# Weight preparation and temporaries in an adaLN linear-attention and MLP kernel: w2 in turn over eleven products, own value tiles for one block, own tiles for modulated rows, one plain group prepared on GpSimd

## The chip, the cores and the metric

The kernel runs on one core of one Trainium2 chip. The metric is the device time of one execution in microseconds, lower being better. The engines are named as the profile names them: PE (TensorE matmul), PEld (its weight loads), DVE (VectorE), ACT (ScalarE), POOL (GpSimd) and SP (SyncE, which issues the DMAs).

## The reference

One block of a conditioned transformer: a modulation from a vector c, a linear attention and an MLP with SiLU. S is 2048 tokens, D is 576, F is 4608, 32 heads of 18.

```python
mod = (_silu(c) @ w_mod).reshape(c.shape[0], 6, 1, -1)
sa, ca, ga, sb, cb, gb = (mod[:, i] for i in range(6))
h = _layernorm(x) * (1 + ca) + sa
x = x + ga * A(h, A_wqkv, A_wo)
h = _layernorm(x) * (1 + cb) + sb
x = x + gb * (silu(h @ B_w1) @ B_w2)

# A: q, k, v = split(h @ wqkv); phi(t) = where(t > 0, t + 1, exp(t)) + 1e-6
# kv = sum_s phi(k) v; z = sum_s phi(k); o = phi(q) kv / (phi(q) z + 1e-6); return o @ wo
```

## The kernel before, in words

All data are 32-bit. Matmuls keep precision by splitting an operand into a high part of type fp32r (a cast on ACT) and a low part (full minus high, a subtraction, mostly on DVE by the helper `sub_hi` at line 62), and by adding three products: high by high, high by low, low by high.

**First stage (to about 225 us).** Modulation, layer norm and transposition of the first block, then k, v and part of the q projections over 16 token tiles (L154), and the sums kv and z.

**Second stage (the loop over s, lines 751 to 787; about 225 to 460 us).** In round s the denominators of token tile s are made (`prod` on POOL at L760, then `q_norm` on DVE), tile s - 1 is transposed, and tile s - 2 goes through `attn_out`, whose weights M are three tiles of the pool `wp`. Every four tiles a layer norm of one block of 512 tokens is finished, and a generator `turn_all(tb)` is queued. It transposes the block in five chunks and modulates them (`turn_chunk_k`: psum to a temporary by ACT at L127, a cast at L693, a subtraction), makes four sums of quarter blocks per pair of chunks on POOL (L712 to L716), splits these into S, and stores everything to the DRAM tensors `hd`, from where the last stage streams it. After its tail chunk the turn appends "units" of the MLP to a filler list, for two of the 18 groups of 256 hidden units, which are done plainly here: two `mlp_up` (L641, silu at L643 into a temporary, cast into `hs` at L644, subtraction) and four `mlp_down` (L655, added to acc at L657) per group. `new_hs()` has a single buffer, and `temp()` two, named `sl`; the turns, the silu outputs and the late q projections all take `temp()`. The weights of the two plain groups come by `load_mlp` in round 4: for each group a DMA of w1, cast and subtraction, the tail (with a POOL memset of part of `wt`, which lies in unused rows of M[2]), a DMA of w2, a multiplication by gb, cast and subtraction; the raw data go through the one `hs` buffer.

**Last stage (from 459.8 us).** The other 16 groups are taken in 8 pairs d, and each pair of groups is multiplied with each of the four blocks b: 32 units. A unit does a seven-product (Winograd) form of both matmuls: seven products `up` in the order 1, 6, 2, 5, 7, 4, 3 (L911) and seven products `down` in the order 1, 7, 2, 4, 5, 6, 3 (L999); the `down` of a unit runs between the `up` products of the next one. After each `up`, adds on DVE (L929, L936, L950) and a silu on ACT follow; `operands` makes the seven operands of `down`, by DVE and POOL (L957, L958 and the sums L969 to L978, which run on POOL). After each `down`, DVE adds a psum bank to U or acc (L1002). The rows of h are streamed by SP into four `rooms`, one fetch per product (L888).

The class `Weights` prepares a pair's weights, with two raw buffers in the pool `wm`. `load1`, `sums1` and `up` make w1 during the unit b = 3 of the pair before, as the program writes it. `load2` is written at the end of that unit. `sums2(s)`, for each of the two groups s of the pair, multiplies w2 by gb (two DVE instructions at L864) and makes four Winograd sums on POOL (L829 to L832); `split2` then makes the cast (L878) and the subtraction (L62) of one of seven parts. Before the change both `sums2` are written ahead of the first product of unit b = 0, and after product q of that unit `down(n)` splits part n = DOWN[q] of both groups. The parts are first read by the `down` products that run during unit b = 1. `w2p` has eight buffers for these parts.

**What sets the order.** In the last stage the order of PE is the program's own (`manual_schedule` for PE). The order of the other engines, and in the second stage that of PE too, comes from a planner that simulates the program when it is built: among what it believes ready, it takes what was written first, and it moves work forward where the data are there. Each engine then executes its queue strictly in that order.

Of the kernel before, what the change touches and what calls it, by code (L numbers as in the profile page):

```python
# [8 lines left out]
F32 = mybir.dt.float32  # L9
F32R = mybir.dt.float32r  # L10
# [5 lines left out]
P = 128  # L16
# [5 lines left out]
def kernel(ctx: ExitStack, tc, A_x, A_wqkv, A_wo, B_x, B_w1, B_w2, c, w_mod, out):  # L22
# [8 lines left out]
    V, A, G, T = nc.vector, nc.scalar, nc.gpsimd, nc.tensor  # L31
# [3 lines left out]
    S, D = x.shape  # L35
# [4 lines left out]
    NB = S // 512  # L40
    KC = D // P
# [5 lines left out]
    G2 = 2  # L47
    NG = F // (G2 * P)

    def f32(ap):  # L50
        return ap.bitcast(F32)
# [9 lines left out]
    def sub_hi(lo, full, hi):  # L61
        return V.tensor_sub(lo, full, f32(hi))  # L62
# [5 lines left out]
    hTa = tc.alloc_tile_pool(name="hTa", bufs=2)  # L68
    wg = tc.alloc_tile_pool(name="wg", bufs=2)
    wp = tc.alloc_tile_pool(name="w", bufs=3)  # L70
    wqp = tc.alloc_tile_pool(name="wq", bufs=1, side="right")
# [9 lines left out]
    bc = {n: pool.tile([P, D], F32, name=f"bc_{n}") for n, pool in (("ga", pa), ("gb", const))}  # L81
# [333 lines left out]
    for t in range(NT):  # L415
        tb, i = t // 4, t % 4
# [28 lines left out]
        for _ in range((0, 2, 1, 1)[t] if t < 4 else 1):  # L445
            q = next(qs)
# [42 lines left out]
    for j, kv in enumerate(kvp):  # L489
        n = min(2, NHC - 2 * j)  # L490
# [27 lines left out]
    M = [wp.tile([P, 4, D], F32R, name="w") for _ in range(3)]  # L518
# [28 lines left out]
    pc = tc.alloc_tile_pool(name="pc", bufs=1, reuse_waits="tile")  # L547
    wg2 = tc.alloc_tile_pool(name="wg2", bufs=2, reuse_waits="tile")
    px = tc.alloc_tile_pool(name="px", bufs=1, reuse_waits="tile")
# [31 lines left out]
    def new_hs(shape=(P, G2, 2, 512), dtype=F32R):  # L581
        t = pc.tile(list(shape), dtype, name="hs")
        return t

    def load_mlp(g, pool, wt):
        f0 = g * FW
        r1 = new_hs((P, KC + 1, FW), F32)
        nc.sync.dma_start(r1[:, 0:KC, :], B_w1[0 : KC * P, f0 : f0 + FW].rearrange("(k p) f -> p k f", p=P))
        for h in range(2):
            nc.sync.dma_start(r1[h * 64 : h * 64 + 64, KC, :], B_w1[KC * P : D, f0 : f0 + FW])  # L590
        w1 = pool.tile([P, 9, FW], F32R, name="w")
        A.copy(w1[:, 0:KC, :], r1[:, 0:KC, :])
        sub_hi(w1[:, KC : 2 * KC, :], r1[:, 0:KC, :], w1[:, 0:KC, :])
        G.memset(f32(wt[64:128, 1, :]), 0.0)
        tail_w(wt, r1[:, KC, :])
        r2 = new_hs((P, G2, D), F32)
        nc.sync.dma_start(r2, B_w2[f0 : f0 + FW, :].rearrange("(j p) d -> p j d", p=P))
        w2 = pool.tile([P, G2, 2, D], F32R, name="w")
        V.tensor_mul(r2, r2, bc["gb"].unsqueeze(1).to_broadcast([P, G2, D]))
        A.copy(w2[:, :, 0, :], r2)  # L600
        sub_hi(w2[:, :, 1, :], r2, w2[:, :, 0, :])
        return w1, w2, wt


# [21 lines left out]
    def temp():  # L626
        t = pc.tile([P, D], F32, name="sl", bufs=2)
        return t[:, :512]
# [29 lines left out]

    def mlp_units(tb, w):

        hs = new_hs()
        up = [lambda j=j: mlp_up(tb, w[0], w[2], hs, j) for j in range(G2)]
        return up, [lambda i=i: mlp_down(4 * tb + i, hs, w[1]) for i in range(4)]

# [32 lines left out]

    def turn_all(tb):

        nonlocal wqp  # L700
        if tb == 0:
            wqp.release()
            wqp = tc.alloc_tile_pool(name="S", bufs=1, side="right", reuse_waits="tile")
        X = h2[tb] = hTa.tile([P, 2 * KC + 2, 512], F32R, name="hT")

        S = [wqp.tile([P, 4, 2 * HT], F32R, name="S", bufs=2) for _ in range(2)]
        for c in range(2):
            t0, t2 = temp(), temp()
            turn_chunk_k(tb, c, t0)
            turn_chunk_k(tb, 2 + c, t2)  # L710
            (a11, a21), (a12, a22) = ((t[:, :HT], t[:, HT:]) for t in (t0, t2))
            G.tensor_sub(a11, a11, a21)  # L712
            G.tensor_add(a21, a21, a22)
            split_s(S[0], c, t0)
            G.tensor_sub(a22, a22, a11)
            G.tensor_sub(a12, a12, a22)  # L716
            split_s(S[1], c, t2)
            yield
        t = temp()
        turn_chunk_k(tb, KC, t)  # L720
        for w in ws:
            up, down = mlp_units(tb, w)
            filler.extend(up + down)
        G.tensor_sub(t[:, :HT], t[:, :HT], t[:, HT:])
        tail_h(X[:, DIFF, :HT], t[:, :HT])
        yield
        store_h(tb, 1, X[:, 0:4, :HT])
        store_h(tb, 2, X[:, 4:9, :HT])
        store_h(tb, 4, X[:, 4:9, HT:])
        store_h(tb, 5, X[:, 8:9, HT:], 4)  # L730
        store_h(tb, 3, X[:, DIFF : DIFF + 1, :HT], 4)
        for n, at in ((7, 0), (5, HT)):
            store_h(tb, n, S[0][:, :, at : at + HT])
        for n, at in ((3, 0), (6, HT)):
            store_h(tb, n, S[1][:, :, at : at + HT])
        yield

    turns, filler = [], []
    qts, xn2, lns = {}, {}, {}

# [7 lines left out]
            if turns and next(turns[0], StopIteration) is StopIteration:  # L748
                turns.pop(0)

    s = 0
    while s < NT + 5 or filler or turns:
        if s < QB - 2:
            filler.append(late_q)
        if s == 4:
            ws = [load_mlp(g, pool, M[2][:, 1 + g, :512].rearrange("p (a f) -> p a f", a=2))
                  for g, pool in enumerate((wg, wg2))]
        if NP0 <= s < NT:
            prod = pb.tile([P, D], F32, name="prod")
            G.tensor_mul(prod, acc[s], z)  # L760
            pns[s] = q_norm(s, prod, pb.tile([P, DX], F32, name="pn", bufs=2))
        t = s - 2
        if t in (5, 9, 13, 17):
            turns.append(turn_all(t // 4 - 1))
        turn_chunk()
        if 0 <= s - 1 < NT:
            qts[s - 1] = q_transpose(pns.pop(s - 1))
        turn_chunk()
        if 0 <= t < NT:
            attn_out(t, qts.pop(t))  # L770
            tb = t // 4
            if t % 4 == 0:
                lns[tb] = LayerNorm(px)
            lns[tb].stats(t % 4, acc[t])
            if t % 4 == 3:
                lns[tb].finish()
                xn2[tb] = [px.tile([P, DX], F32, name="xn", bufs=4) for _ in range(4)]
                for i in range(4):
                    lns[tb].normalise(i, xn2[tb][i], acc[4 * tb + i], A if tb < 2 or i % 2 else V)
        turn_chunk()  # L780
        unit(1 if s < 8 else 2)
        turn_chunk()
        if s % 4 == 0 and s < NT or s > NT:
            unit()
        s += 1
# [2 lines left out]

    for p in (pb, px, wg2, pc, wp, wg, hTa, wqp):
        p.release()
    psB.release()
    psC = tc.alloc_tile_pool(name="psC", bufs=1, space=PSUM, reuse_waits="tile")
# [16 lines left out]

    class Weights:


        def __init__(self, d):
            self.f0, self.wt, self.w1, self.w2 = 2 * d * FW, wts[d % 2], {}, {}
# [50 lines left out]
                self.split2("B12", s, parts[1])  # L867
            self.b2[s] = self.winograd(*parts, [t[:, i] for i in range(3)])

        def down(self, n):  # L870
            for s in range(2):
                self.split2(n, s, self.b2[s][n])

        def split2(self, n, s, src):
            if n not in self.w2:
# [163 lines left out]
    with tc.manual_schedule(engines={mybir.EngineType.PE}):  # L1039
        w = Weights(1)  # L1040
        for f in (w.load1, w.sums1):
            for s in range(2):
                f(s)
        for n in ORDER:
            w.up(n)
        for s in range(2):
            w.load2(s)
        for i in range(4):
            fetch(i)
        for u in U:  # L1050
            G.memset(u, 0.0)
        ws = {1: w}
        before = None
        for m, (d, b) in enumerate(units):
            unit = Unit(m, ws[d])
            final = m + 1 == len(units)
            if b == NB - 1 and d < ND:
                w = ws[d + 1] = Weights(d + 1)
                for f in (w.load1, w.sums1):
                    for s in range(2):  # L1060
                        f(s)
            if b == 0:
                for s in range(2):
                    ws[d].sums2(s)
            for q, n in enumerate(ORDER):
                unit.up(n)
                if before:
                    before.down(q)
                if final:
                    unit.plain_operands(n)  # L1070
                else:
                    unit.operands(n)
                if b == 0:
                    ws[d].down(Unit.DOWN[q])
                if b == NB - 1 and d < ND:
                    ws[d + 1].up(n)
                if m + 3 == len(units) and q == 3:
                    Unit(len(units) - 1, w).add_u((1, 1), (1, 0), (0, 1))
            if b == NB - 1 and d < ND:
                for s in range(2):  # L1080
                    ws[d + 1].load2(s)
            before = unit
        for t in (2, 3, 0, 1):
            unit.plain_down(t)
# [31 lines left out]
```

## Time and profile before

The three runs took 1252.07, 1256.47 and 1259.71 us; the median is 1256.47.

| what | us |
|---|---|
| median of the runs | 1256.47 |
| the profiled execution | 1249.34 |
| its span, first to last instruction | 1247.6 |
| PE busy | 1176.7 (94%) |
| DVE busy | 841.8 (67%) |
| POOL busy | 551.3 (44%) |
| ACT busy | 490.4 (39%) |
| mean granted clock of PE | 0.985 |

The busy shares are means over three different stages. A line of the windows view gives, for one stretch: its length, then for PE, PEld, DVE, ACT and POOL the busy us and the number of instructions that started in it, the granted clock of PE, the busy share of the DMA engines and what they moved in GB/s. A line of the waits view says which engine waited on which instruction, for how long in total, how often, and the longest. A line of the timeline gives start, duration, engine, line, operation, output and input, and in brackets the idle time before it with what ended it. In the groups, "x66 | 48.9, 771" means 66 instructions, 48.9 us in all, 771 ns each.

### The profile page before, as it was taken

The numbers are of one execution on the slowest core, as the hardware profiler recorded it, in microseconds if no ns is written. First come the engines' busy times: TensorE is split into PE (matmuls) and PEld (weight loads), VectorE is DVE, ScalarE is ACT, GpSimd is POOL, SyncE is SP. The second block draws the span as 40 slices with busy tenths as digits, with TensorE's granted clock in tenths as the row PEclk, the third lists the DMA queues.
The fourth block names the chain that finished last, engine by engine and source line by source line (L and its number), as shares of the span: only waits on it lengthen the run. The fifth ranks groups of instructions, "written<-read, shape, count | busy, mean of one in ns | idle before, by whom it ended". The sixth has DMA issues, their size and how long they took to land.

```text
span 1247.6 us, 21904 instructions
## 1 busy us (share of the span) xinstructions
PE 1176.7 (94%) x8809; PEld 1150.5 (92%) x8809; DVE 841.8 (67%) x1309; ACT 490.4 (39%) x944; POOL 551.3 (44%) x471
## 2 busy tenths in 40 slices
PE   5999999897999969999999998999998999998998
PEld 5999999896999768999999998999998999998998
DVE  6665744995775475577578568569568568667764
ACT  5434342234463333343344244244344334333331
POOL 3200000323231435556457457547637736846560
PEclk9999999998999989999999999999999999999999
DMA  9121300224153626566566566565655755655572
GB/s 297 64 67 58 110 1 1 79 88 154 46 176 119 232 88 236 182 214 198 189 213 203 171 224 191 186 194 196 212 180 196 225 181 190 229 182 191 190 247 99
DMA packets 80452, 202.72 MB, mean 162 GB/s; under 512 B 6682, under 2 KB 37662, under 8 KB 80350
## 3 DMA queue, kind: packets, MB, share of 16 engines
q1 hardware_dynamic: 80350, 201.31, 49.2%
q8 instruction: 70, 1.15, 0.4%
q14 instruction: 32, 0.26, 0.1%
HBM read 179.78 MB, written 21.50 MB: 161 GB/s over the span
## 4 chain that ended last, share of the span: by engine, by line
PE 70%; DVE 15%; DMA 8%; POOL 2%; ACT 2%; issue 2%; SPq 1%; DVEq 0%; ACTq 0%; POOLq 0%
PE up L911 23%; PE down L999 21%; PE psK L154 12%; DMA raw<-in_B_w_dram 6%; PE small L641 4%; DVE w L62 4%; PE big L655 3%; PE big L154 3%; DVE raw L864 3%; PE kvp L389 1%; DVE acc L1002 1%; PE down L1034 1%; DVE h L958 1%; DMA acc<-in_A_wqkv_dram 1%; DVE f L950 1%
## 5 line engine op out<-in xcount | busy, mean ns | idle before, releaser
L999 PE MATMUL down<-w,h 128*128 128x288 f32 x2604 | 384.4, 296 | 17.4 <-DVE U L1002 14.0
L911 PE MATMUL up<-room,w 128*128 128x256 f32 x2688 | 384.9, 286 | 13.8 <-DVE f L929 7.6
L999 PEld LDWEIGHTS down<-w,h 128*128 128x128 f32 x2604 | 357.0, 190 | 20.4 <-DVE U L1002 15.4
L911 PEld LDWEIGHTS up<-room,w 128*128 128x128 f32 x2688 | 353.5, 194 | 16.7 <-DVE f L929 9.4
L969 POOL TENSOR_TENSOR s<-f,f 128x512 f32<-128x512 f32 x31 | 40.1, 1292 | 275.2 <-ACT f L951 275.2
L1002 DVE TENSOR_TENSOR acc<-down,acc 128x576 f32<-128x576 f32 x155 | 116.5, 752 | 59.3 <-PE down L999 58.6
L951 ACT ACTIVATE f<-f 128x512 f32<-128x512 f32 x96 | 60.7, 633 | 197.0 <-DVE f L950 197.0
L154 PE MATMUL psK<-w,hT 128*128 128x288 f32 (+2 forms) x896 | 125.5, 298 | 1.7 <-DVE hT L62 1.1
L154 PEld LDWEIGHTS psK<-w,hT 128*128 128x128 f32 x896 | 121.3, 190 | 2.8 <-DVE hT L62 1.6
L957 ACT CAST h<-f 128x512 fp32r<-128x512 f32 x159 | 95.3, 616 | 52.6 <-POOL f L978 47.7
L911 PE MATMUL up<-room,wt 128*128 128x256 f32 x512 | 104.2, 285 | 0.0
L958 POOL TENSOR_TENSOR h<-f,h 128x512 fp32r<-128x512 f32 x62 | 92.6, 1494 | 12.6 <-ACT h L957 12.6
L958 DVE TENSOR_TENSOR h<-f,h 128x512 fp32r<-128x512 f32 x97 | 80.7, 832 | 16.3 <-ACT h L957 15.1
L62 DVE TENSOR_TENSOR w<-raw,w 128x288 fp32r<-128x288 f32 (+1 forms) x130 | 84.6, 683 | 8.4 <-ACT w L852 8.1
L958 POOL TENSOR_TENSOR h<-s,h 128x512 fp32r<-128x512 f32 x62 | 87.2, 1407 | 0.7 <-ACT h L957 0.7
L911 PEld LDWEIGHTS up<-room,wt 128*128 128x128 f32 x512 | 81.0, 195 | 0.0
L950 DVE TENSOR_TENSOR f<-up,f 128x512 f32<-128x512 f32 x64 | 44.0, 688 | 41.5 <-PE up L911 41.4
L1002 DVE TENSOR_TENSOR U<-down,U 128x576 f32<-128x576 f32 x62 | 46.7, 753 | 31.1 <-PE down L999 31.1
L154 PE MATMUL big<-w,qT 128*128 128x288 f32 x448 | 64.6, 299 | 2.4 <-DVE den L509 1.3
L62 DVE TENSOR_TENSOR w<-t,w 128x256 fp32r<-128x256 f32 (+1 forms) x96 | 64.1, 696 | 2.5 <-ACT w L852 2.1
L655 PE MATMUL big<-w,hs 128*128 128x288 f32 x384 | 58.5, 305 | 6.2 <-ACT hs L644 3.9
L154 PEld LDWEIGHTS big<-w,qT 128*128 128x128 f32 x448 | 60.4, 189 | 3.2 <-DVE qT L62 1.6
(184 smaller groups left out, 1616.0 us busy)
## 6 DMA issues: line engine op xcount, KB each, us to landing
room<-hd SPq DMA_DIRECT2D x128, 640.0 KB, 3.9
room<-hd SPq DMA_DIRECT2D x96, 512.0 KB, 3.7
raw<-in_B_w_dram SPq DMA_DIRECT2D x16, 576.0 KB
hd<-S SPq DMA_DIRECT2D x16, 512.0 KB, 4.5
raw<-in_B_w_dram SPq DMA_DIRECT2D x16, 512.0 KB, 3.7
hd<-hT SPq DMA_DIRECT2D x8, 640.0 KB, 8.0
xt<-in_A_x_dram SPq DMA_DIRECT2D x16, 288.0 KB, 5.6
raw<-in_w_mod_dram SPq DMA_DIRECT2D x8, 576.0 KB, 3.7
```

The costliest lines, as they stand in the source:

```text
L62: return V.tensor_sub(lo, full, f32(hi))
L154: T.matmul(ps, xpart(a), wpart(b), start=n == 0, stop=n == len(XW) - 1)
L641: T.matmul(ps, left, right, start=n == 0, stop=n == len(seq) - 1)
L655: T.matmul(ps[:, h, :HALF], hs[:, j, a, tok], w2[:, j, b, h * HALF : (h + 1) * HALF], start=n == 0, stop=n == len(seq) - 1)
L911: T.matmul(ps[:, s], left, right, start=first and s == 0 and m == 0, stop=m == len(seq) - 1, skip_group_check=True)
L950: V.tensor_add(f, ps, more)
L951: A.activation(f, f, AF.Silu)
L957: A.copy(t[:, 0], src)
L958: eng.tensor_sub(t[:, 1], src, f32(t[:, 0]))
L969: G.tensor_add(s1, f[1, 0], f[1, 1])
L999: T.matmul(ps[:, p, :HALF], self.a[n][:, a, s, tok], self.w.w2[n][:, s, b], start=n in (1, 5, 7, 6) and j == 0, stop=j == 5, skip_group_ch ...
L1002: V.tensor_add(dst, ps[:, :, :HALF], dst)
```

## The change

Four edits.

1. `load_mlp` takes an engine for the two subtractions and the multiplication. Group 0 is prepared in round 4 with DVE as before; group 1 is prepared in round 6 with POOL.
2. In the last block (tb = 3) the two groups' `hs` are two new tiles of the pool `wp`, which take the buffers of M[0] and M[1].
3. A new pool `tp` with two buffers `rows` is opened at the first turn. The temporaries of the first pair of chunks (c = 0) and of the tail chunk come from it; those of the second pair come from `temp()` as before.
4. `Weights.down` becomes `down_step(u)`, with u counting products from the start of unit b = 0 (0 to 13, through unit b = 1). Group s = 0 has its `sums2` at u = 0 and its seven splits at u = 0 to 6; group s = 1 has its `sums2` at u = 4 and its splits at u = 4 to 10.

```diff
-    def load_mlp(g, pool, wt):
+    def load_mlp(g, pool, wt, eng):
...
         A.copy(w1[:, 0:KC, :], r1[:, 0:KC, :])
-        sub_hi(w1[:, KC : 2 * KC, :], r1[:, 0:KC, :], w1[:, 0:KC, :])
+        eng.tensor_sub(w1[:, KC : 2 * KC, :], r1[:, 0:KC, :], f32(w1[:, 0:KC, :]))
...
-        V.tensor_mul(r2, r2, bc["gb"].unsqueeze(1).to_broadcast([P, G2, D]))
+        eng.tensor_mul(r2, r2, bc["gb"].unsqueeze(1).to_broadcast([P, G2, D]))
         A.copy(w2[:, :, 0, :], r2)
-        sub_hi(w2[:, :, 1, :], r2, w2[:, :, 0, :])
+        eng.tensor_sub(w2[:, :, 1, :], r2, f32(w2[:, :, 0, :]))
...
     def mlp_units(tb, w):
 
-        hs = new_hs()
+        hs = new_hs() if tb < NB - 1 else wp.tile([P, 4, D], F32R, name="w").rearrange("p a d -> p (a d)")[
+            :, : 4 * 512].rearrange("p (j h t) -> p j h t", j=G2, h=2)
...
     def turn_all(tb):
 
-        nonlocal wqp
+        nonlocal wqp, tp
         if tb == 0:
             wqp.release()
             wqp = tc.alloc_tile_pool(name="S", bufs=1, side="right", reuse_waits="tile")
+            tp = tc.alloc_tile_pool(name="tp", bufs=1, reuse_waits="tile")
+
+        def rows():
+            t = tp.tile([P, 512], F32, name="rows", bufs=2)
+            return t
...
         for c in range(2):
-            t0, t2 = temp(), temp()
+            t0, t2 = (temp(), temp()) if c else (rows(), rows())
...
-        t = temp()
+        t = rows()
         turn_chunk_k(tb, KC, t)
...
-        if s == 4:
-            ws = [load_mlp(g, pool, M[2][:, 1 + g, :512].rearrange("p (a f) -> p a f", a=2))
-                  for g, pool in enumerate((wg, wg2))]
+        if s in (4, 6):
+            g, pool, eng = ((0, wg, V), (1, wg2, G))[s // 2 - 2]
+            ws.append(load_mlp(g, pool, M[2][:, 1 + g, :512].rearrange("p (a f) -> p a f", a=2), eng))
...
     class Weights:
+        LAG = 4
...
-        def down(self, n):
+        def down_step(self, u):
+
             for s in range(2):
-                self.split2(n, s, self.b2[s][n])
+                v = u - s * self.LAG
+                if v == 0:
+                    self.sums2(s)
+                if 0 <= v < 7:
+                    n = Unit.DOWN[v]
+                    self.split2(n, s, self.b2[s][n])
...
-            if b == 0:
-                for s in range(2):
-                    ws[d].sums2(s)
             for q, n in enumerate(ORDER):
...
-                if b == 0:
-                    ws[d].down(Unit.DOWN[q])
+                if b < 2:
+                    ws[d].down_step(7 * b + q)
```

More of the change, by code (lines that the diff above doesn't have):

```diff
@@ L736, in turn_all @@
         yield
+    tp = None
     turns, filler = [], []
@@ L749, in turn_chunk @@
                 turns.pop(0)
-    s = 0
+    s, ws = 0, []
     while s < NT + 5 or filler or turns:
@@ L785 @@
         s += 1
-    for p in (pb, px, wg2, pc, wp, wg, hTa, wqp):
+    for p in (tp, pb, px, wg2, pc, wp, wg, hTa, wqp):
         p.release()
```

## The prediction

> **What bounds the kernel.** I first cut the span at the places where the program changes stage and asked for each engine's busy time there.
>
> ```profile
> core 0: us, PE busy (x) PEld busy (x) DVE busy (x) ACT busy (x) POOL busy (x), PEclk, DMA share, GB/s
> 225.60:459.80 234.20, 211.09 (x1386) 196.64 (x1384) 168.93 (x303) 99.05 (x175) 73.60 (x74) 0.96 0.38 122
> 459.80:480.00 20.20, 17.52 (x119) 17.32 (x120) 10.74 (x19) 7.00 (x16) 12.18 (x14) 0.83 0.75 256
> 480.00:1231.00 751.00, 725.80 (x5690) 720.32 (x5689) 518.03 (x713) 291.37 (x580) 435.88 (x350) 0.99 0.60 197
> ```
>
> TensorE bounds every stage. The change touches the second stage (attention output, two plain MLP groups; 23.1 us of idle PE) and the streamed stage (25.2 us of idle PE). Nothing can be won outside those idle times and the time lost to a lowered clock. So the next view was what PE waited for, first in 225 to 480 us, then in 480 to 1231 us.
>
> ```profile
> PE small L641 <- ACT sl L127: 5.4, 4, 1.8
> PE small L142 <- ACT sl L127: 4.2, 1, 4.2
> PE big L655 <- ACT hs L644: 3.9, 1, 3.9
> PE up L911 <- DVE acc L657: 3.3, 1, 3.3
> ...
> PE big L655 <- DVE acc L657: 2.3, 1, 2.3
> ```
> ```profile
> PE down L999 <- DVE U L1002: 14.0, 7, 2.1
> PE up L911 <- DVE f L929: 7.6, 7, 1.9
> PE down L999 <- DVE acc L1002: 3.1, 7, 0.4
> ```
>
> Columns: total us, times, longest. The second list is 24.7 us in seven equal portions of 3.5: one for each change from one pair of groups to the next. The timeline of one such place shows the cause.
>
> ```profile
> 647.71 1.97 DVE L864 TENSOR_TENSOR raw<-raw,bc_gb 128x576 f32<-128x576 f32 x2 [2.97 <-DMA raw<-in_B_w_dram]
> ...
> 651.02 3.61 DVE L864 TENSOR_TENSOR raw<-raw,bc_gb 128x576 f32<-128x576 f32 x2
> ...
> 655.52 0.74 DVE L1002 TENSOR_TENSOR U<-down,U 128x576 f32<-128x576 f32 x1
> 656.32 1.62 PEld L999 LDWEIGHTS down<-w,h 128*128 128x128 f32 x12 [2.31 <-DVE U L1002]
> ```
>
> The add of U at L1002 empties a bank that PE had filled by 648.6; it comes at 655.5, because the second group's two multiplications (3.61 us) and other w2 work stand ahead of it in DVE's queue. How much w2 work one unit holds follows from the groups by shape:
>
> ```profile
> L62 DVE TENSOR_TENSOR w<-raw,w 128x288 fp32r<-128x288 f32 x66 | 48.9, 771 | 0.3 <-ACT w L878 0.3
> L864 DVE TENSOR_TENSOR raw<-raw,bc_gb 128x576 f32<-128x576 f32 x32 | 42.4, 1362 | 24.1 <-DMA raw<-in_B_w_dram 24.1
> L62 DVE TENSOR_TENSOR w<-t,w 128x288 fp32r<-128x288 f32 x48 | 33.5, 711 | 0.4 <-ACT w L878 0.4
> ```
>
> A unit with b = 0 gives DVE 4 multiplications x 1.362 + 8 subtractions x 0.771 + 6 x 0.711 = 15.9 us of w2 work, beside 7 adds L1002 x 0.752 + 4 adds into f x 0.687 + 3 splits x 0.832 = 10.5. That is 26.4 us, where an undisturbed unit of PE lasts 23.1 (the same piece of the chain of waits starts at 885.31 and 908.41). The excess, 3.3, is what PE loses, 3.5.
>
> Last, the clock in slices of 5 us:
>
> ```profile
> 290.00:295.00 5.00, 3.64 (x10) 2.13 (x8) 3.20 (x4) 2.73 (x5) 2.63 (x3) 0.50 0.30 105
> 445.00:450.00 5.00, 5.00 (x21) 4.87 (x22) 2.50 (x6) 0.33 (x1) 0.00 (x0) 0.50 0.67 220
> ```
>
> After the waits of 4.2 and 3.9 us the granted clock is one half (the slice 295 to 300 has 0.52), so these waits cost more than themselves.
>
> **Part 1, second plain w on POOL and two rounds later.** DVE loses three operations of 2.27, 1.34 and 1.29 us (at 253.4, 261.2 and 265.5): 4.9 us. POOL gets 1024, 1152 and 1152 elements; its rows at 576 elements take 1.43 us, so 2.54 + 2.86 + 2.86 = 8.3 us. PE was busy all the time from 255 to 280, so DVE's relief is worth nothing directly. The three transfers and the zeroing move with them; group 1's w is first read after group 0's unit, that is behind 300 us, some 30 us after the 267 at which it is ready now. What could queue behind the new POOL work is prod (L760), which is made a round ahead, with DVE's den behind it. Value 0. Upper end 8.3 - 4.9 = +3.4, if all of POOL's time stands in DVE's way; lower end -2, the bit that an earlier layer norm gives the turn.
>
> The Trainium skill, SBUF — State Buffer, section Who interferes with whom, says that a VectorE instruction with two SBUF inputs and a GpSimd one that reads SBUF lock each other out, the later one blocking fully. The trace agrees: the 1024-wide subtraction took 1.21 us alone and 2.27 at 253.4, beside a prod that ran to 254.6. By that rule alone the part would cost the whole 3.4 and the end would be 3.4 us later; I stay at 0 because reductions and PSUM reads, much of DVE's work there, have one SBUF input.
>
> **Part 2, own hs tiles for the last plain block.** Before, all hs are one buffer. At 439.4 the cast L644 has to wait for the products before it, ACT meanwhile takes fourteen casts L852 (439.9 to 444.2), and PE stands 3.90 us, then runs at half clock for 5 us (2.5 lost). With two tiles in M's place (M[0], M[1], last read by attn_out of tile 15, long before) the cast needs only its own silu. -6.4. Ends: 0, if another thing is as late (the casts L852 still have to be made ahead of the first streamed product), and -12, if the two acc L657 waits (3.3 + 2.3) go as well.
>
> **Part 3, rows tiles.** At turn 0, PE waits 4.17 + 1.13 + 1.19 us between 285 and 296, and 290 to 300 runs at half clock (half of 3.64 + 4.04 busy, 3.8 lost). The second c's modulation waited at 288.77 for the first c's tile; it needs only the transposes, done at 285.4. The tail's waited until 295.13; with rows it waits for the first c's split, done at 288.2: up to 6.9 us earlier. POOL's four sums (L712 to L716, 0.73 to 1.18 each) stay in series, so I take 4 of the 6.5 and half of the clock: -6. At turn 3 the same tiles cost PE 1.77 + 1.33; half: -1.5. In turns 1 and 2 PE does not wait. Ends 0 and -13.4.
>
> **Part 4, w2 over eleven products.** Group 1's multiplications, sums and splits are four products later. Of its seven splits the last four (two x 0.771, two x 0.711 = 3.0 us) fall into unit b = 1, where DVE has room (15.1 busy of 25 in 675 to 700). Unit 0 keeps 23.4 against 23.1. The first multiplications still wait for their transfer, so the 0.44 stays; of 3.5 I take 2.4 per change, x 7 = -17. Casts on ACT and sums on POOL move along; raw of group 1 is free four products (13 us) later, so its next load on SP's queue is too, with 30 us to spare before b = 3. Ends: -29 (all 24.7, and 4.75 of clock lost in three slices at 0.93 to 0.95), 0 and worse (rivals).
>
> **Sum.** 0 - 6.4 - 7.5 - 17 = -30.9. The profiled execution took 1249.34 us (span 1247.6), 7.1 below the median of 1256.47. 1249.3 - 30.9 = 1218.4, and 7.1 more: **1225**.
>
> **Rivals**, on the same scale.
> A. The edit doesn't spread anything: DVE's order comes from a planner that moves work forward as soon as its data is there (w1 sums written for b = 3 run at 677, in b = 1). Then unit 0 keeps its 26.4 us, and only parts 2 and 3 count: 1256.5 - 13.9 = 1242.6. Against it: what is written later is ranked behind what is ready too, and the U add would pass.
> B. The second stage keeps its waits: the turn is POOL's chain of sums, and the switch to the streamed stage is held by w1's casts. Only part 4: 1239.5.
> C. The wait moves to POOL. Group 1's four sums (0.89 + 1.07 + 1.03 + 1.02 = 4.0 us) now stand before the operand work of b = 0, whose a[7] is ready at 700.5 in an ordinary unit and read by PE at 701.3: 0.8 of slack. 3.2 us x 8 = 26 back: 1251. Against it: POOL idles 6.8 us ahead of that work (663.0 to 669.9).
> D. Slower: group 1's halves come too late for unit 1. Written at product 4, they take 2 x 1.362 + 0.43 + 0.77 = 3.9 us plus DVE's backlog, and are read at product 7, 9.9 us on; a backlog over 6.0 stalls PE. The f add at L929 was 4.5 behind its releaser in the old order (657.8, 662.3). The part decides against the rest from a backlog of 6.0 + 30.9/8 = 9.9; at 12 it costs 6.0 x 8 = 48 against 30.9: 1274.
>
> **Chances.** Forecast 0.45 (own range 1208 to 1240), A 0.16, B 0.13, C 0.11, D 0.15. What a measurement can tell here is about 0.5%, 6.3 us: faster is below 1250.2, slower above 1262.7. The forecast, A and B are faster, 0.74; C is about no change, 0.11; D is slower, 0.15. The range leaves out D and a little below: 1205 to 1262.
>
> **What would show it.** Part 4: the waits for U L1002 and f L929 under 10 us together, the streamed period (L864 to L864, 97.9 now) near 95; A shows as two pairs of L864 still ahead of the first U add, C as PE waiting for POOL h L958, D as PE waiting for L62 or L878 of w. Part 2: no PE wait on hs L644, clock 1.00 around 440. Part 3: no wait over 2 us on sl L127 or rows. Part 1: PE unbroken from 250 to 285. I am wrong if the streamed stage is not shorter by 10 us, or if a wait of a new name takes more than 10.

## The result, and the profile after

The changed kernel takes 1248.4 us (median of 20 runs) where the kernel before takes 1253.8 (median of 20); the ratio is 0.9955 with a 95% interval of 0.9937 to 0.9972. That is 5.6 us faster, inside what the prediction called no change (its bound was 0.5%), where it had forecast 31 us. (The forecast started from 1256.5, the median of three runs.) The profiled execution took 1246.05 us, its span 1244.2.

The six longest waits of PE from 225 to 480 us, in the changed kernel:

```profile
PE down L1015 <- POOL h L974: 3.8, 1, 3.8
PE small L641 <- DVE hT L62: 3.5, 1, 3.5
PE big L655 <- ACT w L644: 3.4, 1, 3.4
PE up L927 <- ACT p L941: 2.0, 1, 2.0
PE up L927 <- DVE acc L657: 1.6, 1, 1.6
PE up L927 <- DVE f L966: 1.4, 1, 1.4
```

The wait of 4.2 us for the modulation at the first turn (L127) is gone and the acc waits shrank from 5.6 to 1.6. But later in the same turn, at 297.0, PE now waits 3.5 us for a subtraction (hT L62). The cast L644, which part 2 was to free, is still 3.4 us late. And the first streamed unit has two new names, POOL h and ACT p, beside a wait for f that the kernel before had there too:

```profile
PE up L911 <- DVE f L950: 2.7, 1, 2.7
```

The waits from 480 to 1231 us:

```profile
PE down L1015 <- DVE U L1018: 13.9, 7, 2.1
PE up L927 <- DVE f L945: 6.5, 5, 1.9
PE down L1015 <- DVE acc L1018: 3.2, 7, 0.5
```

23.6 us against 24.7: part 4, the largest term of the forecast, did nothing. The timeline of the second change of pairs, in the changed kernel, shows why:

```profile
643.86 1.75 PE L1015 MATMUL down<-w,h 128*128 128x288 f32 x12
...
645.32 1.43 DVE L874 TENSOR_TENSOR raw<-raw,bc_gb 128x576 f32<-128x576 f32 x2 [3.59 <-DMA raw<-in_B_w_dram]
...
648.09 3.61 DVE L874 TENSOR_TENSOR raw<-raw,bc_gb 128x576 f32<-128x576 f32 x2
...
652.59 0.75 DVE L1018 TENSOR_TENSOR U<-down,U 128x576 f32<-128x576 f32 x1
...
653.39 2.82 PE L1015 MATMUL down<-w,h 128*128 128x288 f32 x12 [2.06 <-DVE U L1018]
```

Group 1's two multiplications are written four products later now, yet they stand where they stood: ahead of the first add into U. The product that this add empties ended at 645.6, 2.5 us before they began, so this order was planned and is not one of arrival. DVE's queue there, as the two programs were built (the multiplications of both groups, and what follows):

```
before                              after
raw x gb L864 x2 (group 0)          raw x gb L874 x2 (group 0)
acc L1002                           acc L1018
split h L958                        split h L974
raw x gb L864 x2 (group 1)          raw x gb L874 x2 (group 1)
w minus high L62                    w minus high L62
U L1002                             U L1018
```

### The profile page after: what moved, and what is told of

Same layout as the page of the kernel before. It is cut to its first block, busy times and chain, and to the rows that moved or that the text cites. A ratio compares the mean times of both kernels' runs of the same rounds, so it can differ in the third digit from the quotient of the medians.

```text
span 1244.2 us, 21883 instructions
## 1 busy us (share of the span) xinstructions
PE 1177.2 (95%) x8809; PEld 1151.3 (93%) x8809; DVE 850.5 (68%) x1306; ACT 490.9 (39%) x944; POOL 561.1 (45%) x474
## 4 chain that ended last, share of the span: by engine, by line
PE 75%; DVE 14%; DMA 7%; POOL 2%; issue 1%; ACT 1%; SPq 0%; DVEq 0%; POOLq 0%; ACTq 0%
PE up L927 24%; PE down L1015 22%; PE psK L154 12%; DMA raw<-in_B_w_dram 5%; PE small L641 4%; PE big L655 4%; DVE w L62 3%; DVE raw L874 3%; PE big L154 3%; PE kvp L389 1%; PE down L1050 1%; DMA acc<-in_A_wqkv_dram 1%; DVE acc L1018 1%; DVE h L974 1%; DVE hT L62 1%
## 5 line engine op out<-in xcount | busy, mean ns | idle before, releaser
L1015 PE MATMUL down<-w,h 128*128 128x288 f32 x2604 | 386.2, 297 | 21.8 <-DVE U L1018 13.9
L1018 DVE TENSOR_TENSOR acc<-down,acc 128x576 f32<-128x576 f32 x155 | 116.6, 752 | 63.9 <-PE down L1015 63.3
L967 ACT ACTIVATE f<-f 128x512 f32<-128x512 f32 x96 | 60.9, 635 | 194.6 <-DVE f L966 194.5
L62 DVE TENSOR_TENSOR w<-raw,w 128x288 fp32r<-128x288 f32 (+1 forms) x130 | 86.0, 694 | 6.7 <-ACT w L862 6.2
L62 DVE TENSOR_TENSOR w<-t,w 128x256 fp32r<-128x256 f32 (+1 forms) x96 | 65.6, 711 | 2.2 <-ACT w L862 2.0
L1018 DVE TENSOR_TENSOR U<-down,U 128x576 f32<-128x576 f32 x62 | 46.7, 753 | 28.7 <-PE down L1015 28.7
L641 PE MATMUL small<-hT,w 128*128 128x512 f32 x224 | 57.2, 406 | 4.1 <-DVE hT L62 3.5
```

Source lines behind the costliest of these rows:

```text
L641: T.matmul(ps, left, right, start=n == 0, stop=n == len(seq) - 1)
L967: A.activation(f, f, AF.Silu)
L1015: T.matmul(ps[:, p, :HALF], self.a[n][:, a, s, tok], self.w.w2[n][:, s, b], start=n in (1, 5, 7, 6) and j == 0, stop=j == 5, skip_group_ch ...
L1018: V.tensor_add(dst, ps[:, :, :HALF], dst)
```

## The experiments

Each run is told by its ratio to the kernel before, measured beside it on the same chip, with a 95% interval.

### Part 4 alone, and parts 1 to 3 without it

The first kernel has only the fourth hunk of the diff, the second all but it.

> The kernel before with part 4 alone (w2 over eleven products). Theory 1 (the planner moves group 1's work forward again, so that DVE's queue is the old one): ratio to before 0.997 to 1.003, the two pairs of multiplications still ahead of the first add into U, PE's waits for U and for the f add of product 6 again 19 to 23 us in all. Theory 2 (part 4 works and parts 1 to 3 give its gain back): ratio 0.98 to 0.99 and these waits under 10 us.

> Parts 1 to 3 without part 4. Theory 1: the same as the changed kernel, ratio to before 0.993 to 0.998. Theory 2: at or above before, ratio 1.00 or more.

Measured: 1.0009 (0.9999 to 1.0019), and 0.9951 (0.9935 to 0.9967). Part 4 alone leaves 13.9 us of waiting for U and 6.7 for f, and without it the changed kernel's gain is whole. Four products later in the program text is no later in DVE's queue. That the planner believed group 1's data ready before U's product is inferred from this order; the times that it simulated are not on record.

### Group 1 held back by an order edge

Here the text's lateness is made real for the two multiplications, at product 4 and then at product 2. `behind(x)` sets an order edge: what is written inside it can't be placed ahead of x. The x is the latest add into f of the unit.

```diff
-                V.tensor_mul(r2[:, j], r2[:, j], bc["gb"])
+                with behind(hold):
+                    V.tensor_mul(r2[:, j], r2[:, j], bc["gb"])
...
-                    self.sums2(s)
+                    self.sums2(s, hold if s else ())
...
-                    ws[d].down_step(7 * b + q)
+                    ws[d].down_step(7 * b + q, unit.adds[-1:])
```

> The changed kernel, with group 1's two multiplications put by an order edge behind the add into f of product 4 (of its unit), so that they can't be moved forward. Theory 1 (DVE's w2 work in unit b = 0 is what delays the add into U): PE's waits for U and f fall from 20 to under 8 us, the streamed period from 97.3 to about 95, time 12 to 18 us below the changed kernel, ratio to before about 0.983. Rival (the delay comes from the transfer of w2 or from POOL's use of the shared data path, not from the order): the period stays at 97 and the waits keep their sum under the same or another name; PE waiting for the subtraction or cast of w in unit b = 1 would be the price of a late group 1.

> The same with a lag of two products instead of four; the edge then goes to the add into f of product 1. If lateness of group 1 in unit b = 1 costs anything in the run with four, this one is faster than it; if only the load of unit 0 counts, it is slower, with 2 to 6 us more waiting for U and f.

Measured: 1.0003 (0.9982 to 1.0024) and 1.0000 (0.9980 to 1.0020). Neither gains, although the waits for U and f of the old kind are nearly gone. PE's waits in 480 to 1231 us with the edge at product 4:

```profile
PE down L1016 <- ACT h L974: 10.7, 6, 1.8
PE down L1016 <- POOL h L975: 9.1, 7, 4.0
PE down L1016 <- DVE acc L1019: 5.1, 8, 2.2
```

24.9 us under other names. The end of unit b = 0 in that kernel's timeline:

```profile
669.98 3.03 DVE L62 TENSOR_TENSOR w<-raw,w 128x288 fp32r<-128x288 f32 x2
...
672.93 0.68 DVE L967 TENSOR_TENSOR f<-up,f 128x512 f32<-128x512 f32 x1
673.64 0.63 ACT L968 ACTIVATE f<-f 128x512 f32<-128x512 f32 x1 [3.25 <-DVE f L967]
...
675.49 0.78 PE L1016 MATMUL down<-w,h 128*128 128x288 f32 x2 [1.78 <-ACT h L974]
```

Now the subtractions of w2, delayed with the multiplications, stand ahead of the add into f of the last product. The matmuls of that product ended at 667.7, the add comes at 672.9, the silu at 673.6, and the cast of a[7] (the operand of product 7), which stands behind the silu in ACT's queue, makes the `down` of the next unit wait. With the lag of two, PE waits 22.4 us for another add into f (L967), and the time is the same as with four. So it was not enough to move work away from one add: the next add met it. The waits are not all that the edge at product 4 costs. From the first streamed product to the start of the last plain ones PE is idle 29.0 us there against 32.4 in the changed kernel, but the same 5805 matmuls keep it busy 752.1 us against 744.5, at a granted clock of 0.97 against 0.99.

### A cost measured by leaving it out

```diff
-            for j in range(G2):
+            for j in range(G2 if s == 0 else 0):
                 V.tensor_mul(r2[:, j], r2[:, j], bc["gb"])
```

> The changed kernel with group 1's multiplication of w2 by gb left out in the streamed stage (two of four multiplications, 2.7 us of DVE per pair); its output is therefore not the reference's. Theory 1 (DVE's w2 work in unit b = 0 delays the adds that free PE's banks): PE's waits for U and f fall from 20 to under 6 us in all and the time by 12 to 17 us. Rival (POOL's use of the shared path or the transfer sets the wait): they fall by less than 6 us.

Measured: 0.9813 (0.9794 to 0.9831), 1229.7 us, 18 below the changed kernel by the two ratios. The wait for U is gone and that for f remains:

```profile
PE up L927 <- DVE f L945: 7.4, 7, 2.7
```

The fall in time is a little above the 12 to 17 expected, that of the two waits, 13 of 20.4 us, a little below the 14; against the rival, under 6, both decide. DVE's w2 work between the adds is what PE waits for.

### Every w2 operation of DVE behind the add of its step

The list `adds` of a unit now also holds its adds after `down`, so that the edge goes to the add that follows the `down` product of the step.

```diff
-                if v == 0:
+                if u == 2 * s:
                     self.sums2(s)
...
-                V.tensor_mul(r2[:, j], r2[:, j], bc["gb"])
+                with behind(self.hold):
+                    V.tensor_mul(r2[:, j], r2[:, j], bc["gb"])
...
-            sub_hi(w[:, 1], src, w[:, 0])
+            with behind(self.hold):
+                sub_hi(w[:, 1], src, w[:, 0])
...
-                    ws[d].down_step(7 * b + q)
+                    ws[d].down_step(7 * b + q, (before or unit).adds[-1:])
```

> The changed kernel with every w2 multiplication and subtraction on DVE put by an order edge behind the add of the down product of the step it is written at, group 1's multiplications at product 2, splits at 4 to 10 as written. Theory 3 (from the held run: not DVE's total but its order decides; any w2 work that stands ahead of an add into f reaches PE within a unit, by U in b = 0 or by silu, cast and a[7] in b = 1): no wait of PE over 6 us in 480 to 1230 us in all, ratio to before 0.975 to 0.985. Rival (DVE and POOL are full over the two units, and any order only moves the wait): a wait of another name of 18 us or more and a ratio of 0.995 to 1.003.

> The run with order edges on all w2 work, but with both groups in the same seven products again (no lag, multiplications of both at product 0), so that unit b = 0 has all 26.4 us of DVE work by the old rows. Theory 4 (the order edges alone do it, the eleven products add nothing): ratio to before 0.970 to 0.976, as with the lag. Rival (spreading over eleven products is needed too, it only had no effect without the edges): 0.982 to 0.995 and more than 12 us of PE waiting for DVE in the streamed stage.

Measured with the lag: 0.9723 (0.9701 to 0.9745), 1218.9 us, a little beyond the expected gain. Without it: 0.9874 (0.9852 to 0.9896), between theory 4 and its rival, nearer the rival. In the streamed stage PE's waits with the lag are

```profile
PE down L1021 <- POOL h L980: 5.2, 7, 1.3
PE up L933 <- DVE f L972: 2.8, 7, 0.7
```

and without it one line holds nearly all:

```profile
PE up L933 <- DVE f L972: 18.6, 8, 2.9
```

So the full gain needs both: the edges alone are worth 0.8% over the changed kernel, the eleven products another 1.5% once the order makes them real, and nothing without it. The edges also take the first multiplications out of the way of the last acc add of unit b = 3: the waits for acc L1018, 3.2 us in the changed kernel, are no longer on the list.

The waits alone, 8.0 us against 23.6, are about half of what the edges gain. From the first streamed product to the start of the last plain ones the profiles show, in us:

| kernel | length | PE busy | PE idle | granted clock |
|---|---|---|---|---|
| changed | 777.0 | 744.5 | 32.4 | 0.99 |
| group 1 held at product 4 | 781.1 | 752.1 | 29.0 | 0.97 |
| two multiplications left out | 761.7 | 740.3 | 21.4 | 0.99 |
| all w2 behind the adds, with the lag | 747.8 | 735.0 | 12.8 | 1.00 |

Of the 29.1 us by which the last is shorter than the changed kernel, 19.6 are idle time of PE and 9.5 are busy time, at the higher clock. A rival can be put aside here as well: that the edges make the w2 work itself cheaper, by moving it away from POOL. DVE's multiplications and subtractions for w2 take 114.1 us between 480 and 1231 in the changed kernel, 112.9 in the held run and 117.8 in the run with all edges. The total is much the same; what differs is where the work stands.

### The first streamed unit

The changed kernel begins its streamed stage at 450.4 us instead of 459.8, but ends only 3.4 us earlier. From the first streamed product to the first multiplication of the next pair (the first period) it takes 96.7 us (450.39 to 547.07) where the kernel before took 90.2 (459.76 to 549.91). Its timeline in the first unit:

```profile
455.54 1.33 PE L927 MATMUL up<-room,w 128*128 128x256 f32 x6 [2.03 <-ACT p L941]
...
474.92 0.91 POOL L840 TENSOR_TENSOR raw<-raw 128x256 f32<-128x256 f32 x1
...
477.01 1.26 POOL L974 TENSOR_TENSOR h<-f,h 128x512 fp32r<-128x512 f32 x1
...
478.32 2.77 PE L1015 MATMUL down<-w,h 128*128 128x288 f32 x10 [3.81 <-POOL h L974]
```

POOL's sums for the next pair's w1 (L840, moved forward by two to three units) stand among this unit's operands; the operand a[7] is done at 478.3, and PE waits 3.8 us for it. The experiment holds these sums back, behind POOL's last operand of unit b = 1 (`unit.done`):

```diff
-                for f in (w.load1, w.sums1):
+                for s in range(2):
+                    w.load1(s)
+                with behind([pooled]):
                     for s in range(2):
-                        f(s)
+                        w.sums1(s)
...
+            if b == 1:
+                pooled = unit.done
```

> The changed kernel with the POOL sums of the next pair's w1 (written for unit b = 3, moved forward by the planner to b = 0 and 1) put behind POOL's last operand of unit b = 1. Theory for the 7 us that the changed kernel loses in its first streamed unit (these sums stand between the operands of that unit on POOL, PE waits 3.8 us for a[7]): the first unit gains 3 to 6 us, the later periods nothing; ratio to before 0.991 to 0.993. Rival (the unit is held by w2's preparation and the lowered clock): no gain, 0.995.

> Both order edges. Theory 3: the gains add, ratio to before 0.970 to 0.982. Rival: as for spread alone.

Measured: alone 0.9913 (0.9893 to 0.9932), with the order edges on w2 0.9674 (0.9654 to 0.9693), 1211.9 us, the fastest of the study and a little beyond the expected gain. In the first of them the first period takes 94.1 us (450.12 to 544.22), 2.6 less, just short of the 3 to 6 expected, and the later periods 97.05 against 97.26. The wait for a[7] falls only from 3.8 to 2.6, and 3.9 of the 6.5 us lost there stay. The clock is not the reason: what the granted clock lacks of 1, summed over slices of 5 us of the first period, is 3.4 us both here and in the kernel before (5.1 in the changed kernel). PE's waits are the reason: between the first streamed product and 480 us it waits 6.2 us here, for p, f and a[7], and 2.7 in the kernel before. The wait for p is again one of order, here in the changed kernel:

```profile
447.58 0.76 DVE L874 TENSOR_TENSOR raw<-raw,bc_gb 128x576 f32<-128x576 f32 x1 [1.93 <-DMA raw<-in_B_w_dram]
...
454.57 0.43 ACT L894 CAST w<-t 128x288 fp32r<-128x288 f32 x1 [2.23 <-POOL t L839]
454.91 0.58 ACT L941 COPY p<-up 128x512 f32<-128x512 f32 x1
```

ACT's copy of p stands behind a cast of the first pair's w2, which waits for a sum on POOL. That w2 work begins when its transfer has landed, at 447.6 (449.5 in the kernel before). In the kernel before, the streamed stage began ten us after it; now it begins three us after it and meets it. The run with both kinds of edges bears this out in part: there the second multiplications of that w2 come at 455.6 instead of 450.3, the stage begins at 450.4 as in the changed kernel, and the wait for p is gone, while 2.2 us for f and 1.5 for a[7] stay. No run moves this work alone.

Together with the edges, PE's waits from 480 us on are

```profile
PE up L933 <- DVE f L972: 2.8, 7, 0.7
PE down L1021 <- POOL h L980: 0.5, 1, 0.5
```

### Parts 1, 2 and 3, each alone

> The kernel before with part 3 alone (rows tiles). Of the 9.4 us by which the changed kernel starts its streamed stage earlier, this part is expected to bring 3 to 5 (no more wait of 4.2 us for the modulation at the first turn), and, by the theory that the first streamed unit gives most of it back, 0 to 4 us at the end: ratio 0.997 to 1.000.

> The kernel before with part 2 alone (own hs tiles). In the changed kernel the wait on the cast L644 is still 3.4 us of 3.9, so the prediction's reason for this part should fall: the streamed stage starts at most 4 us earlier, ratio 0.997 to 1.001. If the prediction's reason held, the wait would be gone and the ratio 0.995.

> The kernel before with part 1 alone (second plain w on POOL). Expected nothing: ratio 0.998 to 1.002. If POOL's 8.3 us stood in DVE's way, 1.003.

Measured: rows 0.9937 (0.9916 to 0.9957), hs 1.0002 (0.9985 to 1.0019), POOL 1.0006 (0.9988 to 1.0024). Part 3 brings the whole gain of the change, more than the 0.997 to 1.000 expected of it. Where each kernel starts its streamed stage, and where its last plain products begin:

| kernel | streamed stage starts | last products start | between |
|---|---|---|---|
| before | 459.8 | 1230.9 | 771.1 |
| rows alone | 454.2 | 1229.6 | 775.4 |
| hs alone | 456.5 | 1233.7 | 777.2 |
| POOL alone | 461.8 | 1235.1 | 773.4 |
| changed | 450.4 | 1227.5 | 777.1 |

Single profiles of these differ by a few us at both ends, so the ratios decide. Each kernel that starts early also takes longer between; so does the one with POOL alone, which starts late, and the column by itself doesn't show that the early start is the reason. With hs alone the wait at the end of the second stage is there as before, with the new tile in the name, and the timeline shows what it is:

```profile
444.68 1.02 ACT L853 CAST w<-t 128x256 fp32r<-128x256 f32 x3
445.60 0.62 ACT L644 CAST w<-sl 128x512 fp32r<-128x512 f32 x1
...
446.26 6.03 PE L655 MATMUL big<-w 128*128 128x288 f32 x32 [3.38 <-ACT w L644]
```

The silu that the cast needs ran at 441.75, its tile was free; eleven casts of w1 (L853) stand ahead of it in ACT's queue. The wait was one of order, not of a buffer. In the kernel before, too, PE's products ahead of the wait ended at 441.0 (from 439.22, 1.74 us), and the cast came at 444.2, behind the fourteen casts.

## Why the prediction was wrong

**What bounds the kernel** held: PE bounds, its idle time is in the places named, and DVE's w2 work stands ahead of the adds. Leaving two multiplications out and holding all w2 work behind the adds both show it. That the latter comes to 1218.9 us, beside the forecast 1225, is luck: the edges bring 29 us over the changed kernel where part 4 was to bring 17, and of the 13.9 of parts 2 and 3 only 5.6 came in the changed kernel.

**Part 4 is where it failed.** The step reads: "Group 1's multiplications, sums and splits are four products later." They are not: the two queues above are the same, and the streamed stage, which was to be shorter by at least 10 us, is 6 us longer (777.1 for 771.1). Rival A said so ("DVE's order comes from a planner that moves work forward as soon as its data is there"), cited the w1 sums that run two units early, and got 0.16; the sentence against it, that late writing at least ranks group 1 behind the U add, was wrong: in the built queue the multiplications stand ahead of the U add. The trace of before had the warning: work written for b = 3 ran in b = 1, so a shift by four products need not bind.

**The sum of rival A** was too low as well, 1242.6 for 1248.4: it kept 13.9 us for parts 2 and 3. **Part 3** was the right size: 7.5 forecast, 7.9 measured alone (1 - 0.9937, of 1253.8). Alone it also does at the first turn what was forecast, PE's waits there falling by 4.0 us, from 6.5 to 2.5; in the changed kernel the subtraction hT L62 takes most of that back. **Part 2** was sized 6.4 and is worth nothing measurable (up to 1.9 us by its interval). Its end at 0, "the casts L852 still have to be made", is what happened; the step that failed is "the cast needs only its own silu". **Part 1** was 0 and is 0; the end of +3.4 by the lock of the shared path is at the upper edge of its interval (1.0024, 3.0 us) and did not show. Its sign, PE unbroken from 250 to 285, held but for 1.3 us of waiting for the layer norm (xn L119) in the changed kernel.

**Rival B** named a cost that came partly true: most of the early start of the streamed stage is given back, not to w1's casts but in the first unit, 6.5 of 9.4 us, of which holding POOL's sums returned 2.6. **Rival C** appeared where the lag was made real for the multiplications alone: PE waits for a[7], though POOL's sums were not the reason; the add, the silu and the cast ahead of it were late. **Rival D** did not show: in no list of PE's waits is there one for a part of w2.

**Model of DVE's load.** "The excess, 3.3, is what PE loses" named the right work, but its agreement with 3.5 is partly luck: the sum counts four adds into f where a unit has five (160 in 32 units), so that its own rows give 27.1 us and an excess of 4.0. And held, which moves group 1's work out of unit 0's first half, gained nothing, while the same load held behind the adds without any lag gained 0.8% over the changed kernel. The load alone does not set the time; where it stands in the queue does, and then the load.

## What to carry to other kernels

Where a planner orders the queues, moving code does not move work: look in the trace whether other work already runs far from where it is written, compare the built order of the engine's queue, and bind what must be late with an order edge. Bind it behind every operation that frees a bank or feeds the next engine, not behind one of them, since the delayed work will meet the next. Judge such a run by PE's idle and busy time together, since the waits can keep their sum while the clock falls. And an earlier start of a stage is a gain only if what the stage needs from other engines is early too.

## What the runs showed of the hardware

Two multiplications of 576 elements took 1.43 us together where POOL ran for under 0.1 us of them and 3.61 where it ran all the time (the two lines of the changed kernel's timeline above); in the run held at product 4, two subtractions of 288 elements took 3.03 us, while the shortest single ones there took 0.44. The Trainium skill, SBUF — State Buffer, section Who interferes with whom, has the rule for it (two SBUF inputs on VectorE, and a GpSimd instruction that reads SBUF); the traces agree. A plan that counts the short time for each is short by a factor of 2.5 to 3.4 in these lines. Whether the planner counts so is not on record.
